# Batch 0's front in a fused attention and maxout kernel: other projections of k and v, another load order, idle matmuls in the gaps

## The chip, the cores and the metric

One core of one Trainium2 chip. The metric is device time of one execution in microseconds (us), the median of several; an execution's own span in the profile is about 1.8 us shorter. An execution counts as slow when it is over 1.5% above the fastest of the same kernel; those are left out. "Before" is the kernel before the change, "after" the changed one.

## The reference, cut to what matters

```python
# q, k, v: [8, 8, 1024, 64]; E, F: [64, 1024]
k_proj = einsum('ks,bhsd->bhkd', E, k);  v_proj = einsum('ks,bhsd->bhkd', F, v)
attn = softmax(q @ k_proj^T / 8)
x = (attn @ v_proj) as [8192, 512]
out = max(x @ w1, x @ w2, x @ w3) @ w_out        # w1..w3: [512, 768], w_out: [768, 512]
```

All products run in bf16 with float32 accumulation. Batch 0 is special: nothing can be computed until its inputs and the weights have been loaded, so its first half ("chunk 0") is computed in pieces as loads land. Batches 1 to 7 are loaded and their attention computed behind the dense matmuls of the batch before.

## The kernel before

Nearly all loads go through one queue, in this order (batch 0's q, k and v in parts, then the weights; `heads` and `sis` cut out the parts):

```python
load_q(LO, slice(0, SPC)); load_kv(1, LO)      # half of q for chunk 0, half of k
load_q(HI, slice(0, SPC)); load_kv(1, HI)
load_kv(2, slice(0, 2));   load_kv(2, slice(2, 4))     # v by pairs of heads
...
load_w(0, 0)                                   # w1, first half of its rows
load_kv(2, V2); load_kv(2, V3)                 # third and fourth pair of v
load_w(0, 1)
load_w(1, 0); load_w(1, 1)                     # w2
load_w(2, 0)                                   # w3, first half
load_q(ALL, slice(SPC, SI))                    # q for chunk 1
load_w(2, 1)                                   # w3, second half
... # w_out
```

The projections of batch 0, and the order in which the tensor engine (PE) does them:

```python
def k_pair(g):                 # 16 small matmuls, k stationary; gives k_proj transposed at once
    for si in range(SI):
        for hp in range(2):
            matmul(out=t[hp*64:(hp+1)*64, 0:KP], lhsT=k_t[:, 2*g+hp, si, :], rhs=efT[:, si, 0, :], ...)
    copy("v", kpTs[0][:, g, :], t[:, 0:KP], ns, 0.25)
...
idle(11); turn_ef(); q_duo(0); idle(6); k_pair(0); k_pair(1)
... # scores of pairs 0 and 1, idle(2), z(0), q_duo(1), z(1), idle(2)
k_pair(2); k_pair(3)
... # scores of pairs 2 and 3, idle(1)
v_pair(0); z(2); x(0); v_pair(1); z(3); x(1)
```

`idle(n)` is n matmuls of 512 columns that nobody reads; `x(g)` are the value products of pair g and their scaling. Then comes the first up-projection, w1 in one sweep for each of four row blocks (`ct`), w2 and w3 bank by bank. `then` runs what `work` has behind a step:

```python
for ct in range(NCT):                    # w1: 24 matmuls
    for jt in jts:
        up_mm(h[jt][0], 0, 0, 0, jt, (ct,))
        ...
        if jt == 2 or jt == NJT - 1: then((0, ct, jt))
for i in (1, 2):                         # w2, w3: 6 banks of 4 matmuls each
    for jt in jts:
        t, ns = bank(); up_mm(t, i, 0, 0, jt, range(NCT)); ...; then((i, jt))
# work: (0,1,2): v_pair(2);  (0,1,5): x(2), v_pair(3);  (0,2,2): x(3);  (2,0), (2,1): turn q of chunk 1; ...
```

A bank of w3 needs the second half of w3 at its third matmul. I call the first such matmul "w3's third matmul".

The softmax here doesn't subtract the row's maximum and nothing guards it: scores larger than these inputs give would overflow.

Of the kernel before, what the change touches and what calls it, by code (L numbers as in the profile page):

```python
# [9 lines left out]
BF16 = mybir.dt.bfloat16  # L10
# [5 lines left out]
def kernel(  # L16
# [13 lines left out]
    nc = tc.nc  # L30

    B, H, S, D = q.shape
    KP = E.shape[0]
# [4 lines left out]
    P = 128  # L38
    HALF = 64
    SI = 8  # L40
    NCT = DM // P
    NJT = DF // P
    NPAIR = H // 2
    CHUNK = 512
# [5 lines left out]
    const = ctx.enter_context(tc.tile_pool(name="const", bufs=1))  # L50
    loads = ctx.enter_context(tc.tile_pool(name="loads", bufs=1))
    att = ctx.enter_context(tc.tile_pool(name="att", bufs=2))
# [11 lines left out]
    clock = {"pe": 0.0, "s": 0.0, "v": 0.0}  # L64
# [3 lines left out]
    def deal(ns):  # L68
        clock["pe"] = max(clock["pe"], *(free[n] for n in ns))
        for n in ns:  # L70
            assert free[n] < OPEN
            free[n] = OPEN
# [6 lines left out]
    def bank():  # L79
        n = min(range(8), key=lambda n: free[n])  # L80
        deal((n,))
        return psum_t[:, n, :], (n,)

    def pe(dt, wait=0.0):
        clock["pe"] = max(clock["pe"], wait) + dt
        return clock["pe"]

    def runs(eng, ready, dt, ns=()):
        if eng in clock:
            clock[eng] = max(clock[eng], ready + 0.06) + dt  # L90
            for n in ns:
                free[n] = clock[eng]
            return clock[eng]
        return ready + dt
# [3 lines left out]
    def copy(eng, o, i, ns=(), dt=0.65):  # L98
        done = {  # L99
            "v": nc.vector.tensor_copy, "s": nc.scalar.copy, "g": nc.gpsimd.tensor_copy  # L100
        }[eng](out=o, in_=i)
        runs(eng, clock["pe"] if ns else 0.0, dt, ns)
        return done
# [10 lines left out]
    def view(src, b):  # L114
        return src[b].rearrange("h (p si) d -> p h si d", si=SI)


    ident = const.tile([P, P], BF16, name="ident")
# [2 lines left out]
    w_sb = [const.tile([P, NCT, DF], BF16, name=f"w{i}_sb") for i in range(3)]  # L121
    wout_sb = const.tile([P, NJT, DO], BF16, name="wout_sb")

    efT = const.tile([P, SI, 2, KP], BF16, name="efT")

    qkv, qTs, kpTs, vps, pTs, zis, xTs = {}, {}, {}, {}, {}, {}, {}
    last_T = {}
# [4 lines left out]
    q_t, k_t, v_t = (  # L132
        loads.tile([P, H, SI, D], BF16, name=nm) for nm in ("q_t", "k_t", "v_t")
    )
# [7 lines left out]
    def load_kv(i, heads):  # L142
        nc.gpsimd.dma_start(  # L143
            out=qkv[0][i][:, heads], in_=view((q, k, v)[i], 0)[:, heads]
        )
# [3 lines left out]
            out=q_t[:, heads, sis], in_=view(q, 0)[:, heads, sis]  # L149
        )  # L150

    def load_w(i, half):
        cts = slice(half * NCT // 2, (half + 1) * NCT // 2)
        w = (moe_w1, moe_w2, moe_w3)[i].rearrange("(ct p) j -> p ct j", p=P)
        nc.gpsimd.dma_start(out=w_sb[i][:, cts, :], in_=w[:, cts, :])

# [11 lines left out]
    make_identity(nc, ident)  # L168
    nc.vector.memset(ones, 1.0)

    load_w(0, 0)
    load_kv(2, V2)
    load_kv(2, V3)
    load_w(0, 1)
    load_w(1, 0)
    load_w(1, 1)
    load_w(2, 0)
    load_q(ALL, slice(SPC, SI))
    load_w(2, 1)
    nc.gpsimd.dma_start(out=wout_sb, in_=moe_w_out.rearrange("(jt p) m -> p jt m", p=P))  # L180

    def load(b):
# [93 lines left out]
    def proj(b, kv, t, heads, width):  # L276

        for si in range(SI):
            for hh in range(2):
                nc.tensor.matmul(  # L280
                    out=t[hh * HALF:(hh + 1) * HALF, 0:width],
                    lhsT=efT[:, si, kv - 1, :],
                    rhs=qkv[b][kv][:, heads[hh], si, :],
                    start=(si == 0), stop=(si == SI - 1),
                )
        pe(8 * (width * 0.00042 + 0.01))
# [82 lines left out]
    def idle(n):  # L369

        t, ns = bank()
        for _ in range(n):
            nc.tensor.matmul(out=t, lhsT=warm[:, 0:P], rhs=warm, start=True, stop=True)
        free[ns[0]] = pe(n * MM)

    def turn_ef():
        for i in range(2):
            cols = slice(i * S // 2, (i + 1) * S // 2)
            copy("vs"[i], ef_b[:, cols], ef_f[:, cols])
        t, ns = two()  # L380
        t = t.bitcast(BF16)[:, 0]
        src = ef_b.rearrange("k (p si) -> k p si", si=SI)
        for si in range(SI):
            nc.tensor.transpose(
                out=t[:, si * P:(si + 1) * P], in_=src[:, :, si], identity=ident
            )
        pe(0.6)
        for i in range(2):
            copy(
                "vs"[i], efT[:, 4 * i:4 * i + 4].rearrange("p si t k -> p (si t k)"),  # L390
                t[:, i * CHUNK:(i + 1) * CHUNK], ns,
            )

    def k_pair(g):
        t, ns = bank()
        for si in range(SI):
            for hp in range(2):
                nc.tensor.matmul(
                    out=t[hp * HALF:(hp + 1) * HALF, 0:KP],
                    lhsT=k_t[:, 2 * g + hp, si, :],  # L400
                    rhs=efT[:, si, 0, :], start=(si == 0), stop=(si == SI - 1),
                )
        pe(0.45)
        copy("v", kpTs[0][:, g, :], t[:, 0:KP], ns, 0.25)

    def v_pair(g):
        t, ns = bank()
        hs = slice(2 * g, 2 * g + 2)
        proj(0, 2, t, (hs, hs), 2 * D)
        copy("v", vps[0][:, hs].rearrange("a h d -> a (h d)"), t[:, 0:2 * D], ns, 0.3)  # L410

    def q_duo(u):
        t, ns = bank()
        t = t.bitcast(BF16)
        for gg in range(2):
            heads_q(0, 2 * u + gg, range(SPC), t[:, gg * CHUNK:(gg + 1) * CHUNK])
        o = qTs[0].rearrange("a (g si) p -> a g si p", si=SI)
        copy(
            "v", o[:, 2 * u:2 * u + 2, 0:SPC, :],
            t.rearrange("a (g si p) -> a g si p", si=SPC, p=P), ns, 0.7,  # L420
        )
# [3 lines left out]
    def z(g):  # L425
        invert(0, g, *C0, sums(0, g, *C0))

    def x(g):
        scale_x(0, g, *C0, values(0, g, *C0))

    idle(11)
    turn_ef()
    q_duo(0)
    idle(6)
    k_pair(0)
    k_pair(1)
    for g in (0, 1):
        exps(0, g, *C0, scores(0, g, *C0))
    idle(2)
    z(0)  # L440
    q_duo(1)
    z(1)
    idle(2)
    k_pair(2)
    k_pair(3)
    for g in (2, 3):
        exps(0, g, *C0, scores(0, g, *C0))
    idle(1)
    v_pair(0)
    z(2)  # L450
    x(0)
    v_pair(1)
    z(3)
    x(1)

    ffn_sb = ctx.enter_context(tc.tile_pool(name="ffn_sb", bufs=2))
    hTs = {}
# [16 lines left out]
    def up_first(work):  # L474


        def then(key):
            run_later()
            for f in work.get(key, []):
                f()  # L480

        hs = ffn_sb.tile([P, NJT, CHUNK], FP32, name="hs", bufs=1)
        hTs[0, 0] = ffn_sb.tile([P, NJT, CHUNK], BF16, name="hT")
        jts = range(NJT)
        h = [(t[:, n], ns[n:n + 1]) for t, ns in (two(), two(), two()) for n in (0, 1)]
        for ct in range(NCT):
            for jt in jts:
                up_mm(h[jt][0], 0, 0, 0, jt, (ct,))
                if ct == NCT - 1:
                    copy("sv"[jt % 2], hs[:, jt], *h[jt])  # L490
                if jt == 2 or jt == NJT - 1:
                    then((0, ct, jt))
        for i in (1, 2):
            for jt in jts:
                t, ns = bank()
                up_mm(t, i, 0, 0, jt, range(NCT))
                most(hs[:, jt] if i == 1 else hTs[0, 0][:, jt, :], t, ns, hs[:, jt])
                then((i, jt))
# [132 lines left out]
    for b in range(B):  # L631
        p = plan(b)

        def behind(ch, step):
            for f in p.get((ch, step), []):
                f()

        for ch in range(NCHUNK):
            if (b, ch) == (0, 0):
                c1 = (SPC, SPC)  # L640
                up_first({
                    (0, 1, 2): [lambda: v_pair(2)],
                    (0, 1, 5): [lambda: x(2), lambda: v_pair(3)],
                    (0, 2, 2): [lambda: x(3)],
                    (2, 0): [qp(0, (0, 1), *c1)],
                    (2, 1): [qp(0, (2, 3), *c1)],
                    (2, 2): [sc(0, 0, *c1)],
                    (2, 3): [sc(0, 1, *c1)],
                    (2, 5): [za(0, 0, *c1), sc(0, 2, *c1)],
                })  # L650
                run_later()
                behind(0, NJT - 1)
            else:
                for step in range(NJT):
                    up(b, ch, step)
                    behind(ch, step)
            for tt in range(SPC):
                down(b, ch, tt, "v" if (b, ch) == (0, 0) else "s")
                behind(ch, NJT + tt)
# [30 lines left out]
```

## Time and profile before

| | before, first profile |
|---|---|
| median of the first 3 runs | 409.03 us (408.48 to 409.11) |
| profiled execution: time / span | 409.37 / 407.6 us |
| first w1 matmul | 18.39 us |
| w3's third matmul | 33.94 us |
| second half of w3 landed | 32.98 us |

A row of 40 digits on the page cuts the span into slices of 10.2 us; a digit is the busy share in tenths.

```profile
PE   7789999999999999999999999999999999999995
DMA  9999929949926994792899109950510202020202
```

PE idles only in the first three slices, and in those the DMA engines are busy 90% of the time or more. The timeline of PE shows how (start, duration, line, operation, count; in brackets the idle time before it and what ended it):

```profile
18.39 0.50 PE L461 MATMUL banks<-xT,w_sb 128*128 128x512 bf16 x1 [0.43 <-DMA w_sb<-in_moe_w_dram]
19.11 3.09 PE L461 MATMUL banks<-xT,w_sb 128*128 128x512 bf16 x7 [0.22 <-ACT zi L238]
...
24.54 0.64 PE L280 MATMUL banks<-v_t,efT 128*64 128x128 bf16 x16 [0.80 <-DVE xT L249]
...
26.32 8.21 PE L461 MATMUL banks<-xT,w_sb 128*128 128x512 bf16 x36 [0.16 <-issue]
34.46 0.64 PE L291 MATMUL banks<-ident,q_t 128*64 128x128 bf16 x16
```

L461 is the up-projection. Seven matmuls take 3.09 us, 0.43 each, where 36 later ones take 0.22 to 0.23 each: the clock was at half. The table by windows says the same (window, its length, busy us and count of PE, weight loads, DVE, ACT, POOL, then granted clock, DMA share, GB/s):

```profile
18.50:22.00 3.50, 3.28 (x8) 1.06 (x7) 0.21 (x1) 0.38 (x1) 2.04 (x3) 0.51 1.18 209
```

The load of w3's second half was issued at 18.63 us. The DMA view of that moment gives its time to landing (KB, then us), so it landed at 33.0:

```profile
w_sb<-in_moe_w_dram POOLq DMA_DIRECT2D x1, 384.0 KB, 14.4
```

### The profile page before, as it was taken

The page shows a single profiled execution, that of the slowest core. Times are in us where ns is not written, and L with a number is a line of the kernel's source. Part 1 is how long each engine was busy: PE and PEld are TensorE (multiplying, and loading weights), DVE is VectorE, ACT ScalarE, POOL GpSimd, SP SyncE. Part 2 cuts the span into 40 slices and gives each one's busy share as a digit, 9 for nine tenths or more (in the row PEclk, how much of TensorE's full clock was granted, in tenths as well). Part 3 has the DMA queues.
Part 4 walks back from the last instruction along what each step waited for, and adds up shares of the span by engine and source line. Part 5 has one row for each costly group of instructions (what it writes and reads, how often), then busy time and mean ns, then how long its engine had stood idle before and what let it go on. Part 6 is the DMA issues. An engine that isn't in the chain of part 4 may idle for free.

```text
span 407.6 us, 6112 instructions
## 1 busy us (share of the span) xinstructions
PE 393.5 (97%) x2453; PEld 179.7 (44%) x2498; DVE 201.6 (49%) x308; ACT 191.1 (47%) x278; POOL 31.1 (8%) x43
## 2 busy tenths in 40 slices
PE   7789999999999999999999999999999999999995
PEld 3344453444444544444544445444544444444443
DVE  2347665473565527637453555525464363525251
ACT  2611538623764266556544555537535555432322
POOL 7411002002000200200010002000000000000000
PEclk9999999999999999999999999999999999999999
DMA  9999929949926994792899109950510202020202
GB/s 167 207 206 207 216 85 151 252 115 132 244 37 174 183 254 114 124 244 46 182 181 206 52 15 245 206 156 0 131 79 1 103 2 103 2 103 0 105 0 104
DMA packets 58492, 52.30 MB, mean 128 GB/s; under 512 B 25952, under 2 KB 54112, under 8 KB 58464
## 3 DMA queue, kind: packets, MB, share of 16 engines
q0 software_dynamic: 28496, 28.31, 43.7%
q1 hardware_dynamic: 29824, 23.46, 18.1%
q8 instruction: 19, 0.31, 0.3%
q10 hardware_dynamic: 144, 0.13, 0.1%
q14 instruction: 9, 0.07, 0.1%
HBM read 57.15 MB, written 16.78 MB: 181 GB/s over the span
## 4 chain that ended last, share of the span: by engine, by line
PE 90%; DMA 3%; ACT 2%; DVE 1%; POOL 1%; issue 1%; DVEq 0%; ACTq 0%; POOLq 0%
PE banks L461 61%; PE banks L553 19%; PE banks L219 4%; PE banks L280 4%; DMA w_sb<-in_moe_w_dram 3%; PE banks L199 2%; PE banks L291 1%; DVE xT L249 1%; DMA out_dram<-o_sb 0%; ACT zi L238 0%; ACT zl L232 0%; POOL k_t L143 0%; ACT pT L210 0%; POOL q_t L148 0%; POOL v_t L143 0%
## 5 line engine op out<-in xcount | busy, mean ns | idle before, releaser
L461 PE MATMUL banks<-xT,w_sb 128*128 128x512 bf16 x1118 | 256.2, 381 | 2.8 <-issue 0.6
L461 PEld LDWEIGHTS <-w_sb 128*128 128x128 bf16 x1152 | 109.7, 98 | 138.6 <-issue 12.4
L518 DVE TENSOR_TENSOR m<-banks,h1s 128x512 f32<-128x512 f32 x90 | 62.0, 689 | 86.3 <-ACT h1s L514 54.7
L514 ACT COPY h1s<-banks 128x512 f32<-128x512 f32 x90 | 52.4, 582 | 92.9 <-PE banks L461 89.7
L553 PE MATMUL banks<-wout_sb,hT 128*128 128x512 bf16 x369 | 84.8, 380 | 0.7 <-issue 0.2
L249 DVE TENSOR_TENSOR xT<-banks,zi 128x1024 bf16<-128x1024 f32 (+1 forms) x36 | 39.8, 1106 | 77.4 <-ACT zi L238 57.7
L471 DVE TENSOR_TENSOR hT<-banks,m 128x512 bf16<-128x512 f32 x90 | 62.3, 692 | 9.4
L99 ACT COPY o_sb<-banks 128x512 f32<-128x512 f32 (+1 forms) x60 | 34.8, 580 | 53.1 <-PE banks L553 53.0
L553 PEld LDWEIGHTS <-hT 128*128 128x128 bf16 x378 | 36.0, 98 | 45.5 <-issue 3.1
L232 ACT ACTIVATE zl<-banks 128x1024 f32<-128x1024 f32 (+1 forms) x36 | 33.5, 930 | 31.6 <-PE banks L219 31.2
L210 ACT ACTIVATE pT<-banks 128x1024 bf16<-128x1024 f32 (+1 forms) x36 | 33.2, 931 | 11.7 <-PE banks L199 11.7
L238 ACT ACTIVATE zi<-zl 128x1024 f32<-128x1024 f32 (+1 forms) x36 | 34.6, 962 | 1.1
L188 POOL DMA_DIRECT2D q_t<-in_q_dram x7 | 6.1, 877 | 207.1 <-DMA qT<-q_p 71.8
L280 PEld LDWEIGHTS <-efT 128*64 128x64 bf16 x288 | 13.8, 110 | 5.5 <-issue 5.2
L219 PE MATMUL banks<-pT,ones 64*64 64x512 bf16 (+1 forms) x144 | 13.9, 376 | 0.8 <-DVE xT L249 0.3
L219 PE MATMUL banks<-pT,vp 64*64 64x512 bf16 (+1 forms) x144 | 13.3, 356 | 0.4 <-DVE vp L99 0.2
L199 PE MATMUL banks<-qT,kpT 64*64 64x512 bf16 (+1 forms) x144 | 13.2, 360 | 0.5 <-DVE m L518 0.3
L99 DVE CAST vp<-banks 64x256 bf16<-64x256 f32 (+1 forms) x18 | 7.1, 397 | 10.5 <-PE banks L280 5.6
L280 PE MATMUL banks<-v_t,efT 128*64 128x256 bf16 (+1 forms) x176 | 9.9, 254 | 1.9 <-DMA v_t<-in_v_dram 0.8
L219 PEld LDWEIGHTS <-ones 64*64 64x64 bf16 x144 | 4.3, 103 | 14.8 <-issue 14.5
L99 DVE COPY q_p<-q_t 128x1024 bf16<-128x1024 bf16 x24 | 8.5, 420 | 0.0
L99 ACT CAST vp<-banks 64x256 bf16<-64x256 f32 x14 | 5.1, 364 | 7.3 <-PE banks L280 7.1
(44 smaller groups left out, 99.3 us busy)
## 6 DMA issues: line engine op xcount, KB each, us to landing
out_dram<-o_sb SPq DMA_DIRECT2D x30, 512.0 KB, 3.1
k_t<-in_k_dram POOLq DMA_DIRECT2D x7, 1024.0 KB, 14.0
q_t<-in_q_dram POOLq DMA_DIRECT2D x7, 1024.0 KB, 9.4
v_t<-in_v_dram POOLq DMA_DIRECT2D x7, 1024.0 KB, 19.1
w_sb<-in_moe_w_dram POOLq DMA_DIRECT2D x6, 384.0 KB, 13.8
k_t<-in_k_dram POOLq DMA_DIRECT2D x2, 512.0 KB, 8.1
v_t<-in_v_dram POOLq DMA_DIRECT2D x4, 256.0 KB, 12.1
wout_sb<-in_moe_w_out_dram POOLq DMA_DIRECT2D x1, 768.0 KB, 16.9
```

Source lines behind the costliest of these rows:

```text
L99: done = {"v": nc.vector.tensor_copy, "s": nc.scalar.copy, "g": nc.gpsimd.tensor_copy}[eng](out=o, in_=i)
L210: nc.scalar.activation(out=pTs[b, g, lo], in_=t, func=AF.Exp, scale=scale)
L219: nc.tensor.matmul(out=t[hp * HALF:(hp + 1) * HALF, c, 0:nsi * HALF], lhsT=w(rows, hp), rhs=p[rows, hp, :], start=True, stop=True,)
L232: nc.scalar.activation(out=zl, in_=t, func=AF.Ln)
L238: nc.scalar.activation(out=zi, in_=zl, func=AF.Exp, scale=-1.0)
L249: nc.vector.tensor_tensor(out=xTs[b][:, g, lo:lo + nsi, :].rearrange("a (c s) p -> a c (s p)", c=2), in0=t, in1=zi, op=ALU.mult,)
L280: nc.tensor.matmul(out=t[hh * HALF:(hh + 1) * HALF, 0:width], lhsT=efT[:, si, kv - 1, :], rhs=qkv[b][kv][:, heads[hh], si, :], start=(si = ...
L461: nc.tensor.matmul(out=h, lhsT=w_sb[i][:, ct, jt * P:(jt + 1) * P], rhs=xTs[b][:, ct, ch * SPC:(ch + 1) * SPC, :], start=(ct == first), st ...
L471: nc.vector.tensor_tensor(out=o, in0=h, in1=other, op=ALU.max)
L514: nc.scalar.copy(out=h1s, in_=h[0][0])
L518: nc.vector.tensor_tensor(out=m12, in0=h[1][0], in1=h1s, op=ALU.max)
L553: nc.tensor.matmul(out=o_ps, lhsT=hTs[b, ch][:, jt, tt * P:(tt + 1) * P], rhs=wout_sb[:, jt, :], start=(jt == 0), stop=(jt == NJT - 1),)
```

## The change

It wants to start w1 with more of the values ready, fewer interruptions and a full clock. k is projected by quads of heads with E stationary (8 matmuls of 256 columns) and turned afterwards; v is projected with F doubled to 128 columns (8 matmuls instead of 16, and all 128 output partitions filled at once); three v pairs go ahead of w1 and the last one behind nine of its matmuls; w1's second half is loaded in two parts; idle matmuls fill gaps; `at(us)` only moves the model by which PSUM banks are dealt.

```diff
-    load_w(0, 0)
     load_kv(2, V2)
+    load_w(0, slice(0, 2))
     load_kv(2, V3)
-    load_w(0, 1)
+    load_w(0, slice(2, 3))
+    load_w(0, slice(3, 4))
     ... (w2, first half of w3, rest of q, second half of w3: same order as before)
-    def k_pair(g):
-        ... (two heads, k stationary)
+    def k_duo(u):
+            nc.tensor.matmul(out=t[0:KP, 0:4 * D], lhsT=efT[:, si, 0:KP],
+                rhs=k_t[:, 4 * u:4 * u + 4, si, :], ...)
+        copy("v", kp0[u], t[0:KP, 0:4 * D], ns, 0.45)
+    def kt_duo(u):
+        ... (two transposes of kp0[u], a copy into kpTs[0])
     def v_pair(g):
-        proj(0, 2, t, (hs, hs), 2 * D)
+            nc.tensor.matmul(out=t[:, 0:2 * D], lhsT=efT[:, si, KP:3 * KP],
+                rhs=v_t[:, 2 * g:2 * g + 2, si, :], ...)
+    copy("v", efT[:, :, P:P + KP], efT[:, :, KP:P])      (F a second time)
-    idle(6)
-    k_pair(0); k_pair(1)                       (each call on its own line)
+    idle(5)
+    k_duo(0); q_duo(1); kt_duo(0); idle(1)
     ... (scores of pairs 0 and 1, z(0), z(1))
+    k_duo(1); idle(2); kt_duo(1); v_pair(0)
     ... (scores of pairs 2 and 3)
+    x(0); v_pair(1); z(2); z(3); x(1)
+    v_pair(2); idle(2); x(2); idle(1)
-                    (0, 1, 2): [lambda: v_pair(2)],
-                    (0, 1, 5): [lambda: x(2), lambda: v_pair(3)],
-                    (0, 2, 2): [lambda: x(3)],
+                    (0, 1, 2): [lambda: v_pair(3)],
+                    (0, 1, 5): [lambda: x(3)],
```

More of the change, by code (lines that the diff above doesn't have):

```diff
@@ L122 @@
     wout_sb = const.tile([P, NJT, DO], BF16, name="wout_sb")
-    efT = const.tile([P, SI, 2, KP], BF16, name="efT")
+    efT = const.tile([P, SI, 3 * KP], BF16, name="efT")
     qkv, qTs, kpTs, vps, pTs, zis, xTs = {}, {}, {}, {}, {}, {}, {}
@@ L150, in load_q, with load_w @@
         )
-    def load_w(i, half):
-        cts = slice(half * NCT // 2, (half + 1) * NCT // 2)
+    def load_w(i, cts):
         w = (moe_w1, moe_w2, moe_w3)[i].rearrange("(ct p) j -> p ct j", p=P)
@@ L169 @@
     nc.vector.memset(ones, 1.0)
-    load_w(0, 0)
     load_kv(2, V2)
+    load_w(0, slice(0, 2))
     load_kv(2, V3)
-    load_w(0, 1)
-    load_w(1, 0)
-    load_w(1, 1)
-    load_w(2, 0)
+    load_w(0, slice(2, 3))
+    load_w(0, slice(3, 4))
+    load_w(1, slice(0, 2))
+    load_w(1, slice(2, 4))
+    load_w(2, slice(0, 2))
     load_q(ALL, slice(SPC, SI))
-    load_w(2, 1)
+    load_w(2, slice(2, 4))
     nc.gpsimd.dma_start(out=wout_sb, in_=moe_w_out.rearrange("(jt p) m -> p jt m", p=P))
@@ L281, in proj @@
                     out=t[hh * HALF:(hh + 1) * HALF, 0:width],
-                    lhsT=efT[:, si, kv - 1, :],
+                    lhsT=efT[:, si, (kv - 1) * KP:kv * KP],
                     rhs=qkv[b][kv][:, heads[hh], si, :],
@@ L389, in turn_ef, with at @@
             copy(
-                "vs"[i], efT[:, 4 * i:4 * i + 4].rearrange("p si t k -> p (si t k)"),
-                t[:, i * CHUNK:(i + 1) * CHUNK], ns,
-            )
-    def k_pair(g):
+                "vs"[i], efT[:, 4 * i:4 * i + 4, 0:P],
+                t[:, i * CHUNK:(i + 1) * CHUNK].rearrange("p (si x) -> p si x", x=P), ns,
+            )
+    def at(us):
+        clock["pe"] = max(clock["pe"], us)
+    kp0 = {}
+    def k_duo(u):
         t, ns = bank()
         for si in range(SI):
-            for hp in range(2):
-                nc.tensor.matmul(
-                    out=t[hp * HALF:(hp + 1) * HALF, 0:KP],
-                    lhsT=k_t[:, 2 * g + hp, si, :],
-                    rhs=efT[:, si, 0, :], start=(si == 0), stop=(si == SI - 1),
-                )
-        pe(0.45)
-        copy("v", kpTs[0][:, g, :], t[:, 0:KP], ns, 0.25)
+            nc.tensor.matmul(
+                out=t[0:KP, 0:4 * D], lhsT=efT[:, si, 0:KP],
+                rhs=k_t[:, 4 * u:4 * u + 4, si, :],
+                start=(si == 0), stop=(si == SI - 1),
+            )
+        pe(0.9)
+        kp0[u] = att.tile([KP, 4 * D], BF16, name="kp0")
+        copy("v", kp0[u], t[0:KP, 0:4 * D], ns, 0.45)
+    def kt_duo(u):
+        t, ns = bank()
+        t = t.bitcast(BF16)
+        for gg in range(2):
+            nc.tensor.transpose(
+                out=t[:, gg * KP:(gg + 1) * KP],
+                in_=kp0[u][:, gg * P:(gg + 1) * P], identity=ident[0:KP, 0:KP],
+            )
+        pe(0.15)
+        copy(
+            "v", kpTs[0][:, 2 * u:2 * u + 2, :].rearrange("a g k -> a (g k)"),
+            t[:, 0:2 * KP], ns, 0.25,
+        )
     def v_pair(g):
         t, ns = bank()
-        hs = slice(2 * g, 2 * g + 2)
-        proj(0, 2, t, (hs, hs), 2 * D)
-        copy("v", vps[0][:, hs].rearrange("a h d -> a (h d)"), t[:, 0:2 * D], ns, 0.3)
+        for si in range(SI):
+            nc.tensor.matmul(
+                out=t[:, 0:2 * D], lhsT=efT[:, si, KP:3 * KP],
+                rhs=v_t[:, 2 * g:2 * g + 2, si, :],
+                start=(si == 0), stop=(si == SI - 1),
+            )
+        pe(0.5)
+        copy(
+            "v", vps[0][:, 2 * g:2 * g + 2].rearrange("a h d -> a (h d)"),
+            t[:, 0:2 * D], ns, 0.3,
+        )
     def q_duo(u):
@@ L431 @@
     idle(11)
+    at(6.3)
     turn_ef()
     q_duo(0)
-    idle(6)
-    k_pair(0)
-    k_pair(1)
+    copy("v", efT[:, :, P:P + KP], efT[:, :, KP:P])
+    idle(5)
+    at(9.0)
+    k_duo(0)
+    at(10.3)
+    q_duo(1)
+    kt_duo(0)
+    idle(1)
     for g in (0, 1):
@@ L440 @@
     z(0)
-    q_duo(1)
+    idle(1)
     z(1)
+    at(12.8)
+    k_duo(1)
     idle(2)
-    k_pair(2)
-    k_pair(3)
+    kt_duo(1)
+    at(14.3)
+    v_pair(0)
     for g in (2, 3):
         exps(0, g, *C0, scores(0, g, *C0))
-    idle(1)
-    v_pair(0)
-    z(2)
-    x(0)
-    v_pair(1)
-    z(3)
-    x(1)
+    x(0)
+    at(15.5)
+    v_pair(1)
+    z(2)
+    z(3)
+    x(1)
+    at(16.7)
+    v_pair(2)
+    idle(2)
+    x(2)
+    idle(1)
+    at(18.4)
     ffn_sb = ctx.enter_context(tc.tile_pool(name="ffn_sb", bufs=2))
@@ L490, in up_first @@
                     copy("sv"[jt % 2], hs[:, jt], *h[jt])
-                if jt == 2 or jt == NJT - 1:
-                    then((0, ct, jt))
+                then((0, ct, jt))
         for i in (1, 2):
```

## The prediction

> **What bounds the kernel now.** The page gives PE 97% of a 407.6 us span, the chain of waits PE 90%. PE idles almost only at the front: in the row of tenths the first three slices (to 31 us) are under 9, and from 28.3 us on the timeline of PE is dense to the end. The change edits only what stands before that.
>
> **The front (timeline; DMA view, issue plus time to landing).** The 16 DMA engines move about 206 GB/s from 5 us on without a pause, nearly all in one queue in program order. Landings: q 6.4, k 9.0, q 10.3, k 12.8, v pairs 14.1 and 16.6, first half of w1 18.3, v 19.6 and 21.0, rest of w1 22.8, w2 24.7 and 26.6, first half of w3 28.5, rest of q 31.1, second half of w3 33.0, w_out 36.8. The w1 stage runs from 18.39 to 28.3 us, for 24 matmuls that need 24 x 0.216 = 5.2. Lost there: half the clock from about 18.5 to 22.0 (granted 0.51 in that window), eight matmuls at 0.427, 1.6 us; gaps of 0.8, 0.16 and 0.11 for the late pairs; 1.3 for value projections in between.
>
> The Trainium skill, "TensorE: Matmul & The Clock Gate", Part 1, says that the clock has only a full and a half state, judged over windows of about 3.4 us. The trace agrees: one such stretch.
>
> **What the change does.** k by quads: 8 matmuls of 256 columns (estimate 0.9 us), copy 0.45, turn and copy 0.4 per quad, against 0.35 and a copy of 0.24 per pair: longer, but hidden under the v loads. v: 8 matmuls for 16, still 0.5 to 0.6. The third v pair goes ahead of w1 in the queue, so the first half of w1 lands 1.3 us later, at about 19.7. Idle matmuls should keep the full clock. Then nine w1 matmuls 19.7 to 21.7, last v pair to 22.2, three matmuls, values to 23.1, twelve more (w1 parts land at 21.9 and 22.8) to about 25.7: w1 ends 2.6 us sooner.
>
> **How much stays.** w2's second half still lands at 26.6 (stall about 0.5), w2 ends at 31.3, and w3's first bank then waits for w3's second half, which stands behind the same bytes as before and lands at 33.0. Before, it was first needed at 33.94 (w3's third matmul): slack 0.95 us. So the 2.6 us shrink to 0.95; 1.7 become waits for DMA. What follows is unchanged and dense: the total moves by 0.95 us, whether or not the clock stays full.
>
> **Predicted:** 408.1 us, 8 in 10 between 407.3 and 408.9 (before: 409.03). Faster by over 2% 0.01, within 2% 0.98, slower by over 2% 0.01.
>
> **What would show it.** First w1 matmul at about 19.7, released by its DMA; no half-clock window between 16 and 26; last w1 matmul at about 25.7; in the list of waits PE waiting for w2 and w3 weights, together about 1.7 us, the longer just before 33; w3's second half landing within 0.3 of 33.0, its third matmul there; everything later shifted by about 0.95.
>
> **What would make it wrong.** A half-clock window between 18 and 33 us costs up to 1.7 us, of which 1.2 is covered by the wait for w3. The new dealing of PSUM banks may add waits later (some tenths). If w3's second half lands sooner or later than 33.0, the total follows one to one.

## The result, and the profile after

After ran at 409.27 us (408.78 to 409.81, 4 runs) beside 408.94 us for before. The ratio of the fast runs is 1.001, 95% interval 0.9993 to 1.0028: no difference is shown. (A ratio here is the mean time of one kernel's fast runs over that of the other's of the same rounds, so not quite the ratio of the medians quoted.) The predicted 0.95 us gain is absent, and 409.27 lies above the range.

The timeline of PE after (L502 is now the up-projection, L428 the v projection):

```profile
21.51 2.10 PE L502 MATMUL banks<-xT,w_sb 128*128 128x512 bf16 x9
23.45 0.61 PE L428 MATMUL banks<-v_t,efT 128*128 128x128 bf16 x8
23.90 0.81 PE L502 MATMUL banks<-xT,w_sb 128*128 128x512 bf16 x3
24.64 0.30 PE L219 MATMUL banks<-pT,vp 64*64 64x256 bf16 x4
24.87 8.38 PE L502 MATMUL banks<-xT,w_sb 128*128 128x512 bf16 x37
33.87 0.61 PE L502 MATMUL banks<-xT,w_sb 128*128 128x512 bf16 x2 [0.62 <-DMA w_sb<-in_moe_w_dram]
```

The w1 stage is what the change wanted: nine matmuls in 2.10 us at the full clock, no gap, and w1 ends near 27.5 us instead of 28.3. Then PE stands still for 0.62 us until w3's second half has landed, and goes on at 33.87. That is the mechanism that the prediction described. But the landing is at 33.82 us, not at 33.0: the load was issued at 20.73 and took this long (DMA view of that moment):

```profile
w_sb<-in_moe_w_dram POOLq DMA_DIRECT2D x1, 384.0 KB, 13.1
```

w3's third matmul starts at 33.87, against 33.94 before: 0.07 us were won, not 0.95. Yet the span is 0.2 us longer (407.8), so something is lost later as well. Three questions follow. Is the later landing chance or the work of the change? Does before have the 0.95 us of slack that one profile showed? And what is lost behind 34 us?

### The profile page after: what moved, and what is told of

Its sections match the earlier page's. It is cut to its first block, busy times and chain, and to the rows that moved or that the text cites. A ratio compares the mean times of both kernels' runs of the same rounds, so it can differ in the third digit from the quotient of the medians.

```text
span 407.8 us, 5967 instructions
## 1 busy us (share of the span) xinstructions
PE 394.0 (97%) x2381; PEld 180.1 (44%) x2425; DVE 201.5 (49%) x309; ACT 191.2 (47%) x278; POOL 31.4 (8%) x44
## 4 chain that ended last, share of the span: by engine, by line
PE 87%; DMA 7%; ACT 2%; POOL 1%; issue 1%; DVE 1%; DVEq 0%; ACTq 0%; POOLq 0%
PE banks L502 58%; PE banks L593 19%; DMA w_sb<-in_moe_w_dram 7%; PE banks L219 4%; PE banks L280 3%; PE banks L199 2%; PE banks L291 1%; POOL v_t L143 1%; DMA out_dram<-o_sb 0%; ACT zi L238 0%; ACT zl L232 0%; POOL k_t L143 0%; ACT pT L210 0%; POOL q_t L148 0%; DVE hT L512 0%
## 5 line engine op out<-in xcount | busy, mean ns | idle before, releaser
L502 PE MATMUL banks<-xT,w_sb 128*128 128x512 bf16 x1118 | 254.6, 379 | 2.6 <-DMA w_sb<-in_moe_w_dram 0.6
L502 PEld LDWEIGHTS <-w_sb 128*128 128x128 bf16 x1152 | 109.7, 98 | 137.6 <-issue 10.1
L232 ACT ACTIVATE zl<-banks 128x1024 f32<-128x1024 f32 (+1 forms) x36 | 33.5, 930 | 30.9 <-PE banks L219 30.7
L280 PEld LDWEIGHTS <-efT 128*64 128x64 bf16 x224 | 11.7, 110 | 2.7 <-issue 2.7
L373 PE MATMUL banks<-warm 128*128 128x512 bf16 x23 | 8.5, 502 | 1.2 <-DVE warm L166 1.2
```

Source lines behind the costliest of these rows:

```text
L232: nc.scalar.activation(out=zl, in_=t, func=AF.Ln)
L280: nc.tensor.matmul(out=t[hh * HALF:(hh + 1) * HALF, 0:width], lhsT=efT[:, si, (kv - 1) * KP:kv * KP], rhs=qkv[b][kv][:, heads[hh], si, :], ...
L502: nc.tensor.matmul(out=h, lhsT=w_sb[i][:, ct, jt * P:(jt + 1) * P], rhs=xTs[b][:, ct, ch * SPC:(ch + 1) * SPC, :], start=(ct == first), st ...
```

## The experiments

The theory, called A in the expectations: both kernels run into the same wall, the landing of w3's second half, and its time varies from run to run. Rivals: B, before is bound by PE at the front; C, the longer way from k to the scores (2.9 us from the landing of k to the first score in after, 10.87 to 13.78, against 0.8 before) ate the gain; D, the gain is lost later in the kernel. All twelve results agreed with the reference.

### Both kernels again

The edit of these three is none.

> The kernel before, unchanged, for its spread and for the clock of each run. Theory A (both kernels run into the same wall, the landing of the second half of w3; its time varies from run to run with the start of the loads, 32.98 us in the first profile of before and 33.82 in that of after): runs of 408.4 to 409.4 us, ratio 1.000; runs without a half-clock stretch (mean granted clock 0.999 or 1.000) are at most 0.95 us shorter than those with one (0.996), not the 1.6 us that the stretch costs. In this profile the second half of w3 lands anywhere between 32.9 and 34.0. Rival B (before is bound by PE at the front, so the half clock decides): runs with and without the stretch lie 1.6 us apart.

Five fast runs of 408.35 to 410.15 us, ratio to the other runs of before 1.0002. The profile fell into an execution of 824 us and says nothing about the front (see the last section). But each timed run lists its mean granted clock, and the experiments together hold 40 fast runs of before (the runs of the first result list no clock for before). One half-clock stretch of 3.4 us in 407.6 makes a mean of 0.9958; stretches near the end of a run, which some profiles have, take up to 0.0025.

| mean granted clock | runs of before | mean time, us |
|---|---|---|
| 0.998 to 1.000 | 31 | 408.98 |
| 0.997 | 2 | 409.27 |
| 0.995 and 0.996 | 7 | 409.66 |

A full stretch costs before 0.7 us by these means, not 1.6 (where in the run it lay is not listed). The seven slower runs go from 409.04 to 410.39; by their scatter the 95% interval of the cost is about 0.2 to 1.2 us. That is what A expects, by which the wall covers a part, and not B.

> The changed kernel, unchanged. Theory A: in this profile w3's third matmul again starts within 0.1 us of the landing of w3's second half, after a wait of PE of 0.3 us or more, whatever that landing is (33.0 to 34.0); the runs scatter as those of before do, and the mean is within 0.5 us of before on either side. If the landing is near 33.0 here, the start of the loads is chance and not the change; if it is 33.8 again while before has 33.0 again, something in the change delays the loads. Rival C (the longer way from k to the scores, 2.9 us against 0.8, eats the gain): w3's third matmul starts later than its weights land, without a wait for DMA.

409.12 us (408.81 to 409.18), ratio 0.9999 (0.9987 to 1.0011). The w3 wait is there again:

```profile
33.42 0.60 PE L502 MATMUL banks<-xT,w_sb 128*128 128x512 bf16 x2 [1.01 <-DMA w_sb<-in_moe_w_dram]
```

The landing was at 33.37, the same kernel 0.45 us earlier than in its first profile. So the landing moves from run to run. A holds; C does not, since PE waits for DMA and not for its own chain.

> The kernel before again, for one more profile, as the repeat of before was taken in an execution whose clock stayed at half throughout (824 us). Theory A: second half of w3 lands between 32.9 and 33.9; w3's third matmul starts within 0.5 us of that landing in an execution without a half-clock stretch in the w1 stage, and up to 0.95 us after it with one. The span is the start of that matmul plus 373.7 to 373.9, as in the five profiles so far. Rival B: PE never waits for w3 and w3's third matmul is a microsecond or more behind its weights.

409.43 us in the profiled execution. This is the profile that decides about before. Its clock was full in the w1 stage, and:

```profile
19.48 2.12 PE L461 MATMUL banks<-xT,w_sb 128*128 128x512 bf16 x8 [0.30 <-DMA w_sb<-in_moe_w_dram]
...
34.11 0.61 PE L461 MATMUL banks<-xT,w_sb 128*128 128x512 bf16 x2 [0.60 <-DMA w_sb<-in_moe_w_dram]
```

Before waits at the same place, for 0.60 us; the landing was at 34.06, just outside the expected 32.9 to 33.9 (the rest of the span, 373.55 us, missed its 373.7 to 373.9 as narrowly). The half-clock stretch and the early landing of the first profile were both features of one execution; of 40 timed runs 7 had a mean clock as low as that. It was early from its first loads on: the first half of k landed at 8.99 us in it, and at 9.68 to 10.87 in the thirteen other profiles. B falls.

### More to load, and more to compute, ahead of the wall

The load is made longer by 256 KB that nobody uses, in after and in before alike:

```diff
     load_q(ALL, slice(SPC, SI))
+    pad = const.tile([P, 2, SI, D], BF16, name="pad")
+    nc.gpsimd.dma_start(out=pad, in_=view(v, 0)[:, 0:2])
     load_w(2, slice(2, 4))
```

> The changed kernel with 256 KB more (1.28 us of the queue) loaded into an unused tile ahead of the second half of w3. Nothing uses it; the result stays right. Theory A: w3's second half lands 1.28 us later and the total grows by all of it, 1.2 to 1.35 us. Rival C (front bound by the chain through k, loads not binding): growth of at most 0.65 us, or none if the loads had slack.

> The kernel before with the same 256 KB of unused load ahead of the second half of w3. If the slack of 0.95 us that the prediction read from one profile holds in every run, the total grows by about 0.4 us (409.4 to 409.6). Theory A, by which a typical run of before is already close to the wall: growth of 0.9 to 1.9 us (410.0 to 411.0), most of what the same load cost the changed kernel (2.2 us by the medians, of which 1.36 in landings and 0.6 from a later start of the loads in the profile).

After: 411.32 us, ratio to before 1.0056 (1.0043 to 1.0069). Before with the pad: five fast runs of 410.52 to 412.04, median 411.34, ratio 1.0053 (1.0037 to 1.0068). Both grew by 2.2 to 2.3 us over their unpadded medians, so before has no slack of 0.95 us in a typical run. In the list of waits of PE (who waited for whom: us in total, times, longest) for the padded after between 16 and 40 us:

```profile
PE banks L504 <- DMA w_sb<-in_moe_w_dram: 2.7, 2, 2.4
```

The growth was larger than I expected for either kernel (1.2 to 1.35 and 0.9 to 1.9). One part may be the clock: three of the five runs of after and all five of before with the pad had a mean clock of 0.996 or less. Against runs of about the like clock it is 2.0 us for after (409.01 to 411.05, two padded runs) and 1.6 us for before (409.66 to 411.27, where the padded runs have 0.993 to 0.996), still more than 1.28. In the padded after, w3's second half landed at 35.34, 1.97 us later than in the repeat of after, of which the pad's own landing makes 1.28 (32.09 to 33.37); 0.6 us was already there at the last v pair (21.94 against 21.34), before the pad was due. Whether a padded program always starts its loads later, two profiles can't tell; that excess stays open. A slack of 0.95 us would have left before about 0.4 us of growth, and 1.0 us even if its landing was as late by the pad as that of after (1.97).

The other way round, two idle matmuls of 0.43 us together go between w2 and w3 of after:

```diff
                     (0, 1, 5): [lambda: x(3)],
+                    (1, 5): [lambda: idle(2)],
```

> The changed kernel with two idle matmuls (0.43 us of PE) between w2 and w3. Theory A: PE waits there 0.6 to 1.0 us anyway, so the total stays within 0.2 us of 409.1 to 409.2, and the wait for w3 in the profile is shorter by about 0.43 us. Rival C (PE binds): 0.43 us longer, 409.6.

409.11 us, as after (409.12), ratio to before 1.0004. The wait for w3 is 0.5 us instead of 1.0 in the repeat of after at nearly the same landing (33.34):

```profile
33.38 0.61 PE L502 MATMUL banks<-xT,w_sb 128*128 128x512 bf16 x2 [0.46 <-DMA w_sb<-in_moe_w_dram]
```

More work on PE ahead of the wall costs nothing; more bytes ahead of it cost at least their own 1.28 us. That is the wall shown from both sides.

### Single parts of the change

Idle matmuls alone, put into before:

```diff
     x(0)
+    idle(3)
     v_pair(1)
     z(3)
     x(1)
+    idle(2)
```

> The kernel before with five idle matmuls (3 ahead of the second v pair, 2 ahead of w1) where PE waits for loads, so that the clock stays full in the w1 stage. Theory A (the wall covers what a half-clock stretch costs): the median stays within 0.3 us of 409.1, and in the profile PE waits 0.3 to 0.7 us for the second half of w3. The prediction's reading (the stretch and the gaps in the w1 stage put w3 0.95 us behind its landing in every run): 408.1 to 408.4.

408.66 us beside 408.95, ratio 0.9995 (0.998 to 1.001): no difference is shown. In the profile PE waits 0.2 us for w3 (landing 33.50), less than I expected. The result lies between what A and the prediction expected; taken alone it would not decide. Its six runs all have a mean clock of 0.998 or more, and a mean of 408.75 us, where the 31 such runs of before have 408.98. As 33 of 40 runs of before have 0.997 or more without them, six runs can't show that the idle matmuls keep the clock; what they win is at most some tenths.

k by pairs, as in before, put back into after (the v part and the load order kept):

```diff
-    k_duo(0); q_duo(1); kt_duo(0); idle(1)
+    k_pair(0); k_pair(1)
     ... (z(0), q_duo(1), z(1), idle(2))
-    k_duo(1); idle(2); kt_duo(1)
+    k_pair(2); k_pair(3)
```

> The changed kernel with k by pairs as before; load order of the change kept. Theory A: w1 starts up to 1 us sooner, nothing of it is left behind the landing of w3's second half: 409.0 to 409.2, the wait for w3 longer than in the changed kernel (1.0 to 1.6 us, with a wait for w2 of some tenths besides). Rival C (k by quads ate the gain): 408.1 to 408.6.

409.53 us (409.32 to 409.70), 0.3 above the expectation, ratio 1.0014 (0.9999 to 1.003); certainly not the 408.1 to 408.6 of rival C. The landing was at 34.23 in its profile. Two things were not as A expected: w1 did not start sooner (21.85, a full us behind the landing of its weights at 20.85), and the wait for w3 was 0.68 us and not 1.0 to 1.6. The profile shows a likely reason, and something else, too. The window below is a half-clock stretch that lies just ahead of w1, and PE still waits for w3 afterwards:

```profile
17.90:21.30 3.40, 3.40 (x30) 1.96 (x29) 1.28 (x3) 1.91 (x4) 1.78 (x3) 0.51 1.19 207
```

```profile
34.27 0.60 PE L483 MATMUL banks<-xT,w_sb 128*128 128x512 bf16 x2 [0.68 <-DMA w_sb<-in_moe_w_dram]
```

So in this execution the stretch cost nothing at all: the wall covered it. The timed runs say the same: three with a mean clock of 0.995 or 0.996 average 409.59 us, two with 1.000 average 409.45.

### Moving the wall

The second half of w3 goes ahead of the rest of q, and the turning of that q moves one step later; once in after, once in before:

```diff
-    load_q(ALL, slice(SPC, SI))
     load_w(2, slice(2, 4))
+    load_q(ALL, slice(SPC, SI))
...
-                    (2, 0): [qp(0, (0, 1), *c1)],     (and (2,1), (2,2), (2,3))
+                    (2, 1): [qp(0, (0, 1), *c1)],     (and (2,2), (2,3), (2,4))
```

> The changed kernel with the second half of w3 ahead of the rest of q in the load queue, and the turning of that q one step later. Theory A: the wall moves 2.6 us forward, to about 30.4 to 31.2, w3 starts as soon as w2 ends (31.4 to 32.7), PE no longer waits for w3, and the total falls by 0.5 to 1.5 us against the changed kernel: 407.8 to 408.6. Rival C: no change (409.2 plus or minus 0.3), as the front is set by the chain through k. Rival D (the gain is lost later in the kernel): w3 starts earlier, the total stays.

> The kernel before with only the order of loads changed: second half of w3 ahead of the rest of q, the turning of that q one step later. Theory A: executions without a half-clock stretch gain, as the wall moves away and only PE is left, 0.3 to 0.8 us; those with one gain nothing; mean 408.3 to 408.9. The difference to the changed kernel with the same order (408.06) is then what the change's own PE part is worth with the wall moved: 0.3 to 0.8 us. Rival C (the longer way through k in the changed kernel is a loss): this kernel is as fast as or faster than 408.06.

After with the swap: 408.06 us, ratio 0.997 (0.9957 to 0.9984). Before with the swap: 408.52 us, ratio 0.9991 (0.9974 to 1.0007), so its gain is not shown. The wall was at 30.8 and 30.6 us now, and neither profile has a wait for w3. With the wall moved, the change is worth 0.46 us by the medians; the two ratios' intervals overlap a little, so this is likely rather than shown. The clock has a large part in it: before with the swap took 408.08 us on average in its three runs with a mean clock of 0.998 or more (408.98 without the swap) and 409.12 in the three others, 1.0 us more where the unmoved wall left 0.7. These are few runs. The profile of after with the swap fell on an execution of 410.24 us whose clock warmed up late, so its times are not compared. Nor is that execution in the ratio 0.997; with it, the six runs have a mean of 408.32 us against 409.11 for before, 0.998.

Then k by pairs on top of the swap, and last, on top of both, w2's matmuls in two sweeps over its halves:

> The changed kernel with the new load order and k by pairs as before (0.8 us from the landing of k to the scores instead of 2.9). If the chain through k sets the start of w1 there (first w1 matmul 0.4 and 1.06 us behind its weights in two profiles), w1 starts at its landing and the total falls by 0.2 to 0.6 us under 408.06. If not (w1 bound by the landing of its first half), the same within 0.15 us.

```diff
-        for i in (1, 2):
+        h = [bank() for jt in jts]
+        for cts in ((0, 1), (2, 3)):
+            for jt in jts:
+                t, ns = h[jt]
+                up_mm(t, 1, 0, 0, jt, cts)
+                ... (after the second half: the maximum, then((1, jt)))
+        for i in (2,):
```

> A try at a version that beats all: new load order, k by pairs, and w2's matmuls in two sweeps over its halves, so that twelve of them run before its second half lands (the profile of the version without it waited 0.39 us there). Theory A: 0.2 to 0.4 us under 407.8 if that wait is what is left; the same if w3's matmuls then reach its second half (30.9) or the vector engine's 0.69 us per maximum sets the pace, which is likely to take back a part.

With k by pairs: 407.80 us (407.61 to 408.73), ratio 0.9975 (0.996 to 0.9989). w1 starts at 20.09 with its weights landed at 19.98, and the wall is now w2's second half:

```profile
27.03 6.65 PE L483 MATMUL banks<-xT,w_sb 128*128 128x512 bf16 x29 [0.39 <-DMA w_sb<-in_moe_w_dram]
```

The sweeps over halves gave 408.35 us (407.08 to 409.83), ratio 0.9985 (0.9965 to 1.0006): no gain shown, with more scatter. So the best kernels are after with the swap, with or without k by pairs: 0.25 to 0.3% under before, with intervals that exclude 1. Between the two no difference is shown. What k by pairs wins by starting sooner it loses at the clock: with the wall gone, the two of five runs with a mean clock of 0.996 took 408.62 us on average, the other three 407.72. With k by quads none of the six runs was below 0.998 (the mean does not count the late warm-up of one). Over all experiments without the pad, one of 21 runs with k by quads was below 0.997, and eight of 16 with k by pairs put into after; but with the pad it was three of five with k by quads. So the longer projection of k, together with its idle matmuls, probably keeps the clock full more often, which the change wanted; no run tells which of the two does it, and it had no visible effect while the wall stood.

### What is lost behind 34 us

From the first maximum of w3, which follows w3's first bank, to the end of the span, the profiles have:

| kernels | us |
|---|---|
| before: first profile, third, with idle matmuls, with the swap | 373.03, 372.91, 372.86, 373.05 |
| k by pairs in after, the same with the swap | 373.01, 372.94 |
| k by quads: after, its repeat, two idle, pad, swap | 373.33, 373.29, 373.30, 373.20, 373.15 |

Those with k by quads are 0.1 to 0.5 us longer, 0.29 by the means. (The version with halves has w3's first maximum at another place of its schedule and is left out.) Aligned by the last maximum of each of the 96 steps of the up-projections, the repeat of after and the third profile of before run in step, but for short lags of at most 0.35 us that are made up again, until the 72nd, where after falls 0.37 us behind, and 0.25 of it stay. DVE there, in before (third profile) and in after (repeat):

```profile
311.48 0.69 DVE L518 TENSOR_TENSOR m<-banks,h1s 128x512 f32<-128x512 f32 x1
312.27 0.69 DVE L471 TENSOR_TENSOR hT<-banks,m 128x512 bf16<-128x512 f32 x1
```

```profile
310.79 0.69 DVE L558 TENSOR_TENSOR m<-banks,h1s 128x512 f32<-128x512 f32 x1
311.95 0.69 DVE L512 TENSOR_TENSOR hT<-banks,m 128x512 bf16<-128x512 f32 x1 [0.47 <-PE banks L502]
```

The second maximum starts 0.10 us after the first one's end in before, 0.47 us in after. The view puts it down to PE, but the last matmul that it needs started at 311.17 and takes 0.38 us, so both inputs were ready by 311.56. The w_out matmul that reads its result then stands still for about a quarter of a microsecond. From there on all five profiles with k by quads are 0.21 to 0.25 us behind, and none of the others is. Why DVE starts late there, no view shows, and it stays open. So rival D is right for about 0.25 us, and for nothing more.

## Why the prediction was wrong

- *"w1 ends 2.6 us sooner"*: it ended about 0.8 us sooner in the first profile and about 1.9 us sooner in the repeat (27.5 and 26.4 against 28.3; estimates from the start of the last stretch of L502 plus twelve matmuls of 0.216). The loads came later, and w1 started 1.06 and 0.41 us behind the landing of its weights (21.51 against 20.45, 20.43 against 20.02). *"Longer, but hidden under the v loads"* was therefore wrong for the start of w1: PE takes its work in the order of the program, and the longer way from k to the scores pushed v pairs that had landed, and w1, behind it. For the total it did not matter: the version with k by pairs is no faster (409.53).
- *"The 2.6 us shrink ...; the rest become waits for DMA"* and *"w3's third matmul at the landing"*: right in both profiles of after (0.05 us behind the landing). The waits were smaller than the forecast 1.7 us: 0.62 and 1.01 for w3, and of the 0.5 for w2 none in the first profile and about 0.2 in the repeat (two w2 matmuls start 0.44 us apart there, the second at 27.05, right after w2's landing at 27.01; the list of waits leaves out one so short). *"No half-clock window"*: right in both profiles; of the nine timed runs of after one had a mean clock of 0.996.
- *"Before, it was first needed at 33.94 (w3's third matmul): slack 0.95 us"*: **this is the step that failed.** It was read from one execution, which had both an early landing (32.98) and a half-clock stretch. In the third profile of before there is no slack but a wait of 0.60 us, and the padded before grew nearly as much as the padded after. Runs of the full clock (0.998 or more) average 408.98 us for before and 409.01 for after. Before was already at the wall in a typical run, so there was next to nothing for the change to win there.
- *"Lands at 33.0, within 0.3"*: wrong as a fixed number. The landing was 32.98, 34.06 and 33.50 in three profiles of before and of before with idle matmuls, and 33.82, 33.37, 33.34 and 34.23 in four with after's load order. The bytes ahead of it are the same; the scatter is over 1 us and is in both kernels. What makes it stays open.
- *"What follows is unchanged and dense"*: wrong by about 0.25 us in kernels with k by quads. I had named dealing of banks as a risk of some tenths; a loss of this size appeared, but its cause is not shown.
- The sum: the time minus the start of w3's third matmul is 375.4 and 375.3 us in the two fast profiles of before, 375.7 in both of after. With medians of 409.0 and 409.2, that puts the third matmul of a typical run at about 33.6 and 33.5 us (an estimate); with the full-clock means of 408.98 and 409.01 it is 33.6 and 33.3. The change won about 0.1 to 0.3 us there, not 0.95, and lost 0.3 later.

The Trainium skill, "TensorE: Matmul & The Clock Gate", Part 1, says of the clock's windows that they are free-running, that is, not reset when a kernel starts. The traces fit that: the full clock began anywhere from 4.3 to 7.1 us in eleven of the twelve fast profiles though PE's first matmul was always at 1.2, the half-clock stretch of 3.4 us was in one of two fast profiles of before, and a mean clock that fits one in 7 of 40 timed runs. That sentence was a reason to distrust a slack that rested on such a stretch, and I did not draw it.

## What to carry to other kernels

Before you count a gain on a path, look at the landing that stands next in the queue behind it, and measure the slack there in several executions; a slack seen in one profile can be made of that execution's accidents. To find a wall, add work on one side and bytes on the other: two idle matmuls cost nothing here, and 256 KB cost 2.2 us. Where a wall of loads is found, the order of the loads and the compute ahead of them have to change together: neither the rearranged projections alone nor the swapped load alone showed a gain here, both together gave 0.3%.

## What the Trainium skill lacked or had wrong

- "TensorE: Matmul & The Clock Gate", Part 1, has the granted clock of a single busy core at half or full. An execution of the padded before ran with a mean grant of 0.559 and took 684 us. Its up-projection matmuls start 0.40 us apart (835 of 1076 times) or 0.31 (180 times) from the front to the end, where the full clock gives 0.216 and the half-clock stretch gave 0.43; so it is a value between, and not a mixture of the two. It was one execution of that kernel, five others took 410.5 to 412.0 us.
- The same part tells of a clock stuck at a quarter for some 50 us, and says in that sentence that the clock's events in a trace are not reliable. An execution of before took 824 us, with up-projection matmuls spaced 0.44 us and more, about twice the usual 0.216; here a state near half held for the whole span. Its mean grant is listed as 1.000, and the trace holds no record of the clock at all, so that column alone misleads, which agrees with the warning: the two lines below are the list of cores of these two runs.

```profile
core 0: 682.5 us, clock 0.559
```

```profile
core 0: 822.4 us, clock 1.000
```

- The same part gives the warm-up as about 3.4 us of sustained busy time. PE's first matmul was at 1.2 us in every profile; the start of the full clock was at 4.3 to 7.1 us in all but one of the fast profiles, and at 13.8 us in that of after with the swap. PE waited 1.8 us for E and F just before, but it did so in the first profile of after as well, which had the full clock from 6.4 us. The page doesn't say what a gap of this size in the warm-up costs. The idle matmuls before k were at half the clock still, five in 2.31 us:

```profile
9.89 2.31 PE L373 MATMUL banks<-warm 128*128 128x512 bf16 x5
```

- "DMA: Bandwidth & Descriptors" has no rate for loads that convert. The loads here read float32 and write bf16, and the windows show about 206 GB/s written, which makes about 412 read (an estimate from the types).
- The same page has no figure for how much the landing of identical transfers scatters between executions: 32.98 to 34.23 us here, behind 33 us of saturated queue. Nor has any page what an instruction fetch among the loads costs them. The DMA view of after between 18.6 and 20 us shows one of 16 KB, whose packet took 0.96 us (4.3% of 16 engines' 1.4 us); that such packets shift landings was not tested.

```profile
q8 instruction: 1, 0.02, 4.3%
```
